# Second layer of six experts by Strassen's algorithm: seven block products in place of eight

## The chip, the cores and the metric

The kernel runs on one core of a Trainium2 chip. The metric is the device time of one execution in microseconds (us); smaller is better. In the profile's rows the engines are called PE (TensorE, matrix products) and PEld (its loading of stationary operands), DVE (VectorE), ACT (ScalarE), POOL (GpSimd) and SP (SyncE, which here only issues transfers).

## What is computed

Three stages follow each other. A gated linear attention over 4 batches of 8 heads, 768 steps and 48 channels gives x, 3072 rows of 384. The first mixture sends every row through all 8 experts. The second mixture sends each row through its top two of 8 experts. The change touches the first mixture:

```python
def _moe_ref(x, w_gate, w1, w2):          # x: 3072 x 384, w1: 8 x 384 x 1024, w2: 8 x 1024 x 384
    logits = x @ w_gate
    ...
    out = np.zeros((N, D), dtype=np.float32)
    for e in range(E):
        h = np.maximum(x @ w1[e], 0.0)
        ye = h @ w2[e]
        out += P[:, e:e + 1] * ye
    return out.astype(np.float32)
```

P is a table of 3072 x 8 weights, made from the logits by repeated normalising of rows and columns.

## The kernel before

Every fp32 operand of an expert is held as two fp16 parts, high and low, and a product a·b is summed from three matmuls in fp32: high·high, high·low and low·high. So each 128-deep step of a product is three matmuls, and every matmul loads a stationary operand of its own.

The first mixture runs expert by expert (e = 0 to 7), and in each expert over 6 blocks (nb) of 512 rows. A block has two parts. The first layer, `g1` (L130 to L133), makes the hidden values of 128 channels f for the 512 rows: 9 matmuls of 512 columns into one PSUM bank (L130), then ACT writes the high part of the rectified result (`hh`, L132) and DVE the low part (`hl`, L133). There are 8 such units to a block. The second layer, `g2` with `mm2` (L161), takes 128 rows at a time: 24 matmuls of 384 columns (8 channel groups by 3) into one bank, with hidden values as the stationary operand; then DVE multiplies by the row's weight in `Pm` and adds to `acc` in SBUF (L179). There are 4 such units to a block, and they are written between the `g1` units of the next block, so that PE has other work while ACT and DVE finish a block's hidden values. PSUM is one pool of 8 banks, which is used in turn.

Weights come in 7 pieces for each expert: SP issues a load of 512 KB or 384 KB into a staging tile `wst` (L86, L90), ACT makes the high part (L101) and DVE the low part (L102). `w_queue` lists these steps, and `w_pump` takes one of them whenever the planner's clock, which `pump(t)` moves by the time that the author set for each unit, is 2.2 past the last. `w_need` takes all that are left before an expert begins. POOL does nothing for experts 1 to 6.

Expert 0 of the first mixture is partly interleaved with the attention. During expert 7 the rows of x are written to DRAM for the second mixture, which gathers rows by expert; its first layer is L676, its second is `mm2` again, its transposes are L665, and its results are scattered to the output by POOL (L688). Each engine works through its own instructions strictly in the order in which they are written.

## Time and profile before

| | |
|---|---|
| median of 3 runs | 2121.61 us (2121.56 to 2124.22) |
| profiled execution | 2124.83 us, of which the span of instructions 2122.8 us |
| granted TensorE clock, mean | 0.994 |
| PE busy in the span | 2065.0 us (97%) |
| DVE, ACT, POOL busy | 898.8, 564.5, 248.0 us |

A busy time is the union of the times of an engine's instructions. Matmuls are pipelined, so the duration of one matmul is longer than its share of the engine; what one costs is read from the distance between starts.

### The profile page before, as it was taken

What the parts mean: (1) busy time and instruction counts of PE and PEld (TensorE: products, weight loads), DVE (VectorE), ACT (ScalarE), POOL (GpSimd) and SP (SyncE); (2) the same over time, 40 slices, a digit from 0 to 9 for tenths busy, and PEclk for the clock granted to TensorE, in tenths of its full rate; (3) what the DMA queues carried; (4) which work ended last, traced back from release to release, by engine and by line L of the source; (5) the groups of instructions that cost most, each with busy time, mean ns of one, the idle gap of its engine ahead of it and who ended that gap; (6) DMA issues with size and microseconds to landing.
All of it is one profiled execution on the core that took longest, in us unless ns stands there. A gap on an engine that the chain in (4) does not pass through costs nothing. (4 is left out here: it accounts for less than half of the span.)

```text
span 2122.8 us, 31270 instructions
## 1 busy us (share of the span) xinstructions
PE 2065.0 (97%) x13531; PEld 1196.5 (56%) x13531; DVE 898.8 (42%) x1697; ACT 564.5 (27%) x965; POOL 248.0 (12%) x236
## 2 busy tenths in 40 slices
PE   6999999999999999999999999999999999999996
PEld 5888655555555555555555555555555555555553
DVE  8889664232322322232232223223336655444431
ACT  5554412111211211121121112112333434332320
POOL 2434200000000000000000000000000232333332
PEclk9999999999999999999999999999999999999998
DMA  6332112100200100020010001001001435344431
GB/s 209 109 99 95 55 38 100 73 1 1 75 1 1 50 10 1 1 60 1 1 49 11 1 1 50 1 1 47 24 23 52 124 67 134 72 90 96 95 65 24
DMA packets 61820, 106.49 MB, mean 50 GB/s; under 512 B 10980, under 2 KB 44029, under 8 KB 61680
## 3 DMA queue, kind: packets, MB, share of 16 engines
q1 hardware_dynamic: 50256, 85.05, 12.6%
q0 software_dynamic: 11136, 18.89, 5.1%
q8 instruction: 107, 1.75, 0.3%
q10 hardware_dynamic: 288, 0.52, 0.1%
q14 instruction: 33, 0.27, 0.0%
HBM read 85.17 MB, written 21.63 MB: 50 GB/s over the span
## 5 line engine op out<-in xcount | busy, mean ns | idle before, releaser
L161 PE MATMUL bank<-wh,hh 128*128 128x384 f16 (+1 forms) x1984 | 647.6, 326 | 0.0
L161 PE MATMUL bank<-wl,hh 128*128 128x384 f16 (+1 forms) x1984 | 647.6, 326 | 0.0
L161 PE MATMUL bank<-wh,hl 128*128 128x384 f16 (+1 forms) x1984 | 647.5, 326 | 0.0
L161 PEld LDWEIGHTS <-hh 128*128 128x128 f16 (+1 forms) x3968 | 385.0, 98 | 264.7 <-issue 3.7
L132 ACT ACTIVATE hh<-bank 128x512 f16<-128x512 f32 x352 | 210.2, 597 | 1062.2 <-PE bank L130 1061.3
L133 DVE SCALAR_TENSOR_TENSOR hl<-bank,hh 128x512 f16<-128x512 f32 x352 | 243.2, 691 | 514.4 <-ACT hh L132 514.1
L130 PE MATMUL bank<-xl,wh 128*128 128x512 f16 x1056 | 400.2, 379 | 0.0
L130 PE MATMUL bank<-xh,wh 128*128 128x512 f16 x1056 | 400.2, 379 | 0.0
L130 PE MATMUL bank<-xh,wl 128*128 128x512 f16 x1056 | 400.2, 379 | 0.0
L130 PEld LDWEIGHTS <-wh 128*128 128x128 f16 x2112 | 206.3, 98 | 228.7
L161 PEld LDWEIGHTS <-hl 128*128 128x128 f16 (+1 forms) x1984 | 195.0, 98 | 128.0 <-issue 0.5
L179 DVE SCALAR_TENSOR_TENSOR acc<-bank,Pm,acc 128x384 f32<-128x384 f32 x168 | 103.7, 617 | 369.1 <-PE bank L161 369.0
L130 PEld LDWEIGHTS <-wl 128*128 128x128 f16 x1056 | 103.3, 98 | 124.6
L964 POOL MEMSET acc<- 128x768 f16 x8 | 5.9, 737 | 1276.7 <-DVE x L501 1276.7
L678 ACT ACTIVATE hh<-bank 128x384 f16<-128x384 f32 (+1 forms) x128 | 66.3, 518 | 238.1 <-PE bank L676 232.9
L688 POOL DMA_INDIRECT out_dram<-acc,ix x56 | 94.3, 1684 | 284.2 <-DVE acc L687 235.3
L102 DVE SCALAR_TENSOR_TENSOR wl<-wst,wh 128x768 f16<-128x768 f32 (+1 forms) x112 | 118.7, 1068 | 19.7 <-ACT wh L101 17.7
L679 DVE SCALAR_TENSOR_TENSOR hl<-bank,hh 128x384 f16<-128x384 f32 (+1 forms) x128 | 75.3, 589 | 118.6 <-ACT hh L678 108.9
L676 PEld LDWEIGHTS <-wh 128*128 128x128 f16 x768 | 72.6, 98 | 55.9 <-issue 3.7
L101 ACT ACTIVATE wh<-wst 128x768 f16<-128x768 f32 (+1 forms) x112 | 100.9, 927 | 3.5 <-DMA wst<-in_moe_w_dram 3.5
L676 PE MATMUL bank<-xh,wh 128*128 128x448 f16 (+1 forms) x384 | 98.8, 339 | 1.4 <-ACT xh L666 1.4
L676 PE MATMUL bank<-xl,wh 128*128 128x448 f16 (+1 forms) x384 | 98.9, 339 | 0.0
(178 smaller groups left out, 1516.1 us busy)
## 6 DMA issues: line engine op xcount, KB each, us to landing
wst<-in_moe_w_dram SPq DMA_DIRECT2D x48, 512.0 KB
wst<-in_moe_w_dram SPq DMA_DIRECT2D x64, 384.0 KB
la<-in_alpha_dram SPq DMA_DIRECT2D x24, 260.0 KB
lk<-in_k_dram SPq DMA_DIRECT2D x24, 256.0 KB
lq<-in_q_dram SPq DMA_DIRECT2D x22, 256.0 KB
lv<-in_v_dram SPq DMA_DIRECT2D x24, 192.0 KB
out_dram<-zero SPq DMA_DIRECT2D x6, 768.0 KB
xd<-x SPq DMA_DIRECT2D x24, 192.0 KB
```

The source lines that it names most:

```text
L101: nc.scalar.activation(t[0][:, s], st[:, :n], AF.Copy, scale=SW)
L102: nc.vector.scalar_tensor_tensor(t[1][:, s], st[:, :n], SW, t[0][:, s], op0=OP.mult, op1=OP.subtract)
L130: nc.tensor.matmul(p, w1s(e, a, kc, f), x[:, kc, s], start=(n == 0), stop=(n == 3 * KC - 1))
L132: nc.scalar.activation(hh[:, f, :], p, AF.Relu)
L133: nc.vector.scalar_tensor_tensor(hl[:, f, :], p, 0.0, hh[:, f, :], op0=OP.max, op1=OP.subtract)
L161: nc.tensor.matmul(p, a[:, f, s], w2s(x, b, f), start=(f + n == 0), stop=(f == FC - 1 and n == 2))
L179: nc.vector.scalar_tensor_tensor(acc[:, T, :], p, Pm[:, T, e:e + 1], acc[:, T, :], op0=OP.mult, op1=OP.add)
L676: nc.tensor.matmul(p, w1s(x, a, kc, f), xt[:, b * KC + kc, :], start=(i == 0), stop=(i == 3 * KC - 1))
L678: nc.scalar.activation(hh[:, f, :n], p, AF.Relu)
L679: nc.vector.scalar_tensor_tensor(hl[:, f, :n], p, 0.0, hh[:, f, :n], op0=OP.max, op1=OP.subtract)
L688: nc.gpsimd.indirect_dma_start(out=out, out_offset=bass.IndirectOffsetOnAxis(ap=ix, axis=0), in_=y, in_offset=None, bounds_check=N - 1, oo ...
L964: nc.gpsimd.memset(r, 0.0)
```

## The change

For experts 1 to 6 (`STR`) the second layer of a block of 512 rows is done as one product of 2 x 2 blocks. The hidden values A of the block are cut in halves of 256 rows and halves of 512 channels (A11, A12, A21, A22), the weights B in halves of 512 channels and of 192 columns. Seven products of sums of blocks (Winograd's form of Strassen's algorithm) give the same output as the eight products of blocks. The sums of A (S1 to S4) are made in the new first layer `s1`, those of B (T1, T3, T2N, N4) in `w_sums` once for each expert.

- `s1` does for a pair of channel groups (j and j + 4) what two `g1` units did, and then makes four sums: DVE forms them in fp32 straight from PSUM, ACT rounds all four to the high part in one instruction of 1024 elements, and POOL makes the low part with one subtraction of 1024 elements.
- `s2` does 7 products for each of 2 groups of rows, 12 matmuls of 192 columns each (4 channel groups by 3). The sums of products are formed by accumulating further products in the same bank and adding the bank to `acc` in between: 5 additions for each group. The banks are of a new pool of 4 (`long`); the other 4 stay for `s1`.
- `s2` of a block is written as one piece behind the first `s1` of the next block.
- The weight steps are three units deep in place of two (load, sums on POOL, split), spaced 6.0 on the planner's clock in the first mixture, with a staging tile twice as often reused (2 tiles in place of 3), and the low and high parts of a w2 piece are 1344 wide in place of 768.
- To make room, hidden values, staging of expert 0 and some tiles of the attention lie elsewhere in SBUF, the setup of the second mixture (`m2_setup`) stands in expert 7 in place of the end of the attention, and the zero writes (`zq`) stand in expert 7.

```diff
+    STR = range(1, E - 1)
+    ND = DM // 2
+    B11, B21, B22, T1, T3, T2N, N4 = range(7)
...
+    def w_sums(x, i, st):
+        if x not in STR or i < KC:
+            return
+        g = nc.gpsimd
+        b = st[:, :4 * ND].rearrange("p (a b d) -> p a b d", a=2, b=2)
+        c = [st[:, k * ND:(k + 1) * ND] for k in range(8)]
+        g.tensor_sub(st[:, 4 * ND:6 * ND].rearrange("p (a d) -> p a d", a=2), b[:, :, 1, :], b[:, 0, :, :])
+        g.tensor_sub(c[6], c[4], c[3])
+        g.tensor_add(c[7], c[2], c[6])
...
+    A11, A12, A22, S1, S2, S3, S4 = range(7)
+    def s1(e, nb, j, between):
...
+        for f in (j, j + FC // 2):
+            p = bank([128, 512])
+            n = 0
+            for kc in range(KC):
+                for a, x in ((0, xh), (0, xl), (1, xh)):
+                    nc.tensor.matmul(p, w1s(e, a, kc, f), x[:, kc, tok], start=(n == 0), stop=(n == 3 * KC - 1))
+                    n += 1
+            b.append(p)
+            if f == j:
+                t = SS["pool"].tile([128, 5, 256], F32, name="ss")
+                a11, a21 = p[:, :256], p[:, 256:]
+                nc.scalar.activation(left(e, nb, j, 0, A11), a11, AF.Relu)
+                nc.scalar.activation(t[:, 0], a21, AF.Relu)
+                stt(left(e, nb, j, 1, A11), a11, left(e, nb, j, 0, A11), OP.subtract)
+                stt(t[:, 3], a11, t[:, 0], OP.subtract)
+                between(1.97)
+        a12, a22 = p[:, :256], p[:, 256:]
+        nc.scalar.activation(lefts(e, nb, j, 0, A12, 2), p, AF.Relu)
+        stt(t[:, 1], a22, t[:, 0], OP.add)
+        stt(t[:, 2], a11, t[:, 1], OP.subtract)
+        stt(t[:, 4], a12, t[:, 2], OP.add)
+        stt(lefts(e, nb, j, 1, A12, 2), p, lefts(e, nb, j, 0, A12, 2), OP.subtract)
+        sums = t[:, 1:].rearrange("p a n -> p (a n)")
+        nc.scalar.activation(lefts(e, nb, j, 0, S1, 4), sums, AF.Copy)
+        nc.gpsimd.tensor_sub(lefts(e, nb, j, 1, S1, 4), sums, lefts(e, nb, j, 0, S1, 4))
+        between(1.97)
+    def s2(e, nb, Pm, between):
...
+        def prod(out, q, aop, wop, start=False, stop=False):
+            n = 0
+            for j in range(FC // 2):
+                for a, b in ((0, 0), (0, 1), (1, 0)):
+                    nc.tensor.matmul(out, left(e, nb, j, a, aop)[:, q * 128:(q + 1) * 128], w2t(e, b, wop, j),
...
+            a, c = long_bank([128, DM]), long_bank([128, DM])
+            BA[q], BC[q] = a, c
+            t, u = TT[q]
+            prod(a[:, Rt], q, A11, B11, start=True)
+            add(t, 0, ND, a[:, Rt])
+            prod(c[:, L], q, A22, N4, start=True)
+            prod(c[:, Rt], q, S1, T1)
+            add(u, 0, DM, c)
+        for q in range(2):
+            a, (t, u) = BA[q], TT[q]
+            prod(a[:, Rt], q, S2, T2N)
+            prod(a[:, L], q, A12, B21)
+            add(t, 0, DM, a)
+        for q in range(2):
+            a, c, (t, u) = BA[q], BC[q], TT[q]
+            prod(c[:, Rt], q, S4, B22, stop=True)
+            add(t, ND, ND, c[:, Rt])
+            prod(a[:, Rt], q, S3, T3, stop=True)
+            add(u, 0, DM, a[:, None, Rt].to_broadcast([128, 2, ND]))
...
-        for i in range(NW + 1):
+        for i in range(NW + 2):
             def f(i=i):
+                if i > 1:
+                    w_split(x, i - 2, st_.pop((x, i - 2)))
+                if 0 < i <= NW:
+                    w_sums(x, i - 1, st_[x, i - 1])
                 if i < NW:
                     st_[x, i] = w_load(x, i)
-                if i > 0:
-                    w_split(x, i - 1, st_.pop((x, i - 1)))
...
-            w_at[0] = clk[0] + 2.2
+            w_at[0] = clk[0] + (6.0 if len(W) < E else 2.2)
```

How the order on PE changes is seen where a first-layer unit of an expert of the first mixture meets the second layer of the block ahead. Before (`wh`, `wl` are the two parts of the weights, `hh`, `hl` those of the hidden values):

```order
L130 MATMUL bank<-xh,wl_7045 128x512
L161 LDWEIGHTS hh
L161 MATMUL bank<-wh_7044,hh 128x384
L161 LDWEIGHTS hh
L161 MATMUL bank<-wl_7045,hh 128x384
L161 LDWEIGHTS hl
L161 MATMUL bank<-wh_7044,hl 128x384
```

After (`wt` holds all parts and sums of the weights, `hid` all parts and sums of the hidden values):

```order
L272 MATMUL bank<-xh,wt_72 128x512
L306 LDWEIGHTS hid
L306 MATMUL long<-wt_72,hid 128x192
L306 LDWEIGHTS hid
L306 MATMUL long<-wt_72,hid 128x192
L306 LDWEIGHTS hid
L306 MATMUL long<-wt_72,hid 128x192
```

Each matmul still has a load of its own ahead of it. Before, 24 such pairs follow each other and then 18 of the first layer; now 168 pairs of half the width follow each other and then 72 of the first layer.

On DVE, one second layer of a block and the first layer of the next, before (two `g1` units, then one addition, four times over):

```order
L133 SCALAR_TENSOR_TENSOR hl<-bank,hh 128x512 x2
L179 SCALAR_TENSOR_TENSOR acc<-bank,Pm,acc 128x384
L133 SCALAR_TENSOR_TENSOR hl<-bank,hh 128x512 x2
L179 SCALAR_TENSOR_TENSOR acc<-bank,Pm,acc 128x384
L133 SCALAR_TENSOR_TENSOR hl<-bank,hh 128x512 x2
L179 SCALAR_TENSOR_TENSOR acc<-bank,Pm,acc 128x384
```

After: the last `s1` of a block (j = 3), the first of the next block (j = 0), and the ten additions of the `s2` between:

```order
L295 SCALAR_TENSOR_TENSOR hid<-bank,hid 128x256
L295 SCALAR_TENSOR_TENSOR ss<-bank,ss 128x256 x4
L295 SCALAR_TENSOR_TENSOR hid<-bank,hid 128x512
L295 SCALAR_TENSOR_TENSOR hid<-bank,hid 128x256
L295 SCALAR_TENSOR_TENSOR ss<-bank,ss 128x256 x4
L295 SCALAR_TENSOR_TENSOR hid<-bank,hid 128x512
L316 SCALAR_TENSOR_TENSOR acc<-long,Pm,acc 128x192
L316 SCALAR_TENSOR_TENSOR acc<-long,Pm,acc 128x384
L316 SCALAR_TENSOR_TENSOR acc<-long,Pm,acc 128x192
L316 SCALAR_TENSOR_TENSOR acc<-long,Pm,acc 128x384 x3
L316 SCALAR_TENSOR_TENSOR acc<-long,Pm,acc 128x192
L316 SCALAR_TENSOR_TENSOR acc<-long,Pm,acc 128x384
```

On POOL, which before has no row between the setup of the second mixture and its first gathers, the subtractions of `s1` (L291, four to a block) now stand with the sums of the weights (L127 to L129, four times for each expert) among them:

```order
L291 TENSOR_TENSOR hid<-ss,hid 128x1024 x9
L127 TENSOR_TENSOR wst<-wst 128x384
L128 TENSOR_TENSOR wst<-wst 128x192
L129 TENSOR_TENSOR wst<-wst 128x192
L127 TENSOR_TENSOR wst<-wst 128x384
L128 TENSOR_TENSOR wst<-wst 128x192
L129 TENSOR_TENSOR wst<-wst 128x192
L291 TENSOR_TENSOR hid<-ss,hid 128x1024
L127 TENSOR_TENSOR wst<-wst 128x384
L128 TENSOR_TENSOR wst<-wst 128x192
L129 TENSOR_TENSOR wst<-wst 128x192
L291 TENSOR_TENSOR hid<-ss,hid 128x1024 x2
```

The nine subtractions are the two blocks 0 and 1 and the first `s1` of block 2; the first two groups of weight sums so stand in the `s2` behind it, the third between j = 1 and j = 2 of block 2, the fourth behind its j = 3.

## Rows read from the trace of the kernel before

**Rows 1.** The profile's first part: busy us, share of the span, instructions.

```profile
PE 2065.0 (97%) x13531; PEld 1196.5 (56%) x13531; DVE 898.8 (42%) x1697; ACT 564.5 (27%) x965; POOL 248.0 (12%) x236
```

**Rows 2.** Busy time of the engines in an attention stretch, experts 1 to 6, second mixture.

```profile
core 0: us, PE busy (x) PEld busy (x) DVE busy (x) ACT busy (x) POOL busy (x), PEclk, DMA share, GB/s
50.00:100.00 50.00, 47.81 (x649) 40.66 (x646) 43.85 (x69) 25.22 (x52) 19.26 (x20) 1.00 0.32 101
300.00:1400.00 1100.00, 1100.00 (x5936) 580.84 (x5935) 335.66 (x500) 202.98 (x324) 0.00 (x0) 1.00 0.07 24
1600.00:2050.00 450.00, 441.55 (x3084) 265.39 (x3083) 228.85 (x619) 157.59 (x260) 138.00 (x103) 1.00 0.39 92
```

**Rows 3.** PE's timeline about one second-layer unit: start us, duration us; 24 L161 between.

```profile
1004.65 0.38 PE L130 MATMUL bank<-xh,wl 128*128 128x512 f16 x1
1004.87 0.33 PE L161 MATMUL bank<-wh,hh 128*128 128x384 f16 x1
...
1008.77 0.38 PE L130 MATMUL bank<-xh,wh 128*128 128x512 f16 x1
```

**Rows 4.** PE's timeline about one first-layer unit pair: 18 L130 up to 1004.87.

```profile
1000.99 0.38 PE L130 MATMUL bank<-xh,wh 128*128 128x512 f16 x1
```

**Rows 5.** PE's timeline in the attention: 18 L147 of 128 columns up to 31.19.

```profile
30.19 0.22 PE L147 MATMUL bank<-xh,wh 128*128 128x128 f16 x1
...
31.19 0.28 PE L271 MATMUL bank<-ident,ks 128*128 128x128 f32 x1
```

**Rows 6.** PEld groups: count, busy us, mean ns of one, idle before.

```profile
L161 PEld LDWEIGHTS <-hh 128*128 128x128 f16 x3840 | 371.6, 98 | 256.3 <-issue 1.2
L147 PEld LDWEIGHTS <-wl 128*128 128x128 f16 x240 | 24.0, 100 | 6.0 <-issue 3.8 <-DVE wl L102 0.5
```

**Rows 7.** DVE groups by shape, the same columns.

```profile
L133 DVE SCALAR_TENSOR_TENSOR hl<-bank,hh 128x512 f16<-128x512 f32 x352 | 243.2, 691 | 514.4 <-ACT hh L132 514.1
L179 DVE SCALAR_TENSOR_TENSOR acc<-bank,Pm,acc 128x384 f32<-128x384 f32 x168 | 103.7, 617 | 369.1 <-PE bank L161 369.0
L102 DVE SCALAR_TENSOR_TENSOR wl<-wst,wh 128x768 f16<-128x768 f32 x64 | 60.6, 954 | 5.6 <-ACT wh L101 4.0
L292 DVE TENSOR_TENSOR am<-acc,am 128x1024 f16<-128x1024 f32 x24 | 29.2, 1218 | 13.0 <-ACT am L291 12.9
L153 DVE SCALAR_TENSOR_TENSOR hl<-bank,hh 128x256 f16<-128x256 f32 x16 | 6.4, 410 | 0.0
L383 DVE TENSOR_TENSOR Pm<-Pm,rs 128x192 f32<-128x192 f32 x8 | 2.9, 358 | 0.3
```

**Rows 8.** ACT groups by shape.

```profile
L132 ACT ACTIVATE hh<-bank 128x512 f16<-128x512 f32 x352 | 210.2, 597 | 1062.2 <-PE bank L130 1061.3 <-PE bank L569 0.9
L101 ACT ACTIVATE wh<-wst 128x768 f16<-128x768 f32 x64 | 51.5, 835 | 1.5 <-DMA wst<-in_moe_w_dram 1.5
L291 ACT ACTIVATE am<-acc 128x1024 f16<-128x1024 f32 x24 | 25.4, 1056 | 19.7 <-POOL acc L284 19.7
L152 ACT ACTIVATE hh<-bank 128x256 f16<-128x256 f32 x16 | 6.2, 385 | 8.3 <-PE bank L147 8.2
```

**Rows 9.** POOL groups by shape.

```profile
L258 POOL TENSOR_TENSOR g<-acc,ce 64x192 f32<-64x192 f32 x40 | 45.7, 1143 | 99.1 <-DVE ce L247 68.4 <-PE bank L271 24.5 <-PE bank L305 4.7
L489 POOL IOTA vv<- 128x192 bf16 x1 | 0.7, 669 | 0.0
L467 POOL IOTA irow<- 128x128 bf16 x1 | 0.2, 238 | 0.0
```

**Rows 10.** POOL's one-input instruction of 512 elements, L284: ns least/median/most.

```profile
L284 POOL TENSOR_SCALAR_AFFINE_SELECT acc<-acc x48: 629/719/1643, 11.3 to 236.1; 128x512 f32<-128x512 f32 x48
```

**Rows 11.** What PE waited for from 1600 to 2050 us: total us, times, longest.

```profile
PE bank L665 <- DMA acc<-xd,ix: 5.5, 7, 1.6
PE bank L629 <- DVE rhs L622: 1.6, 1, 1.6
PE bank L676 <- ACT xh L666: 1.4, 1, 1.4
```

More of the change, by code (lines that the diff above doesn't have):

```diff
@@ L188 @@
     C2 = C + 2
-    LQ = [ap_.tile([128, NP, C], F32, name=f"lq{i}") for i in range(NL)]
+    spare = SPARE[0].bitcast(F32)
+    LQ = [spare[:, i * NP * C:(i + 1) * NP * C].rearrange("p (r c) -> p r c", r=NP) for i in range(NL)]
     LK = [ap_.tile([128, NP, C], F32, name=f"lk{i}") for i in range(NL)]
@@ L192 @@
     NV = 3
-    LV = [ap_.tile([128, H, D], F32, name=f"lv{i}") for i in range(NV)]
+    lv = [spare[:, NL * NP * C + i * H * D:NL * NP * C + (i + 1) * H * D] for i in range(2)]
+    lv.append(HID[:, 2 * FC * 512:2 * FC * 512 + 2 * H * D].bitcast(F32))
+    LV = [x.rearrange("p (h d) -> p h d", h=H) for x in lv]
     order = [(c, b) for c in range(NC) for b in range(B)]
@@ L748, in overflow @@
             for i in range(4):
-                st = sg.tile([128, 1024], F32, tag="wst", name="wst")
+                st = stage()
                 for a in range(2):
@@ L809 @@
                 gq += [("g2", e, nb, j) for j in range(4)]
+        elif e in STR:
+            stream.append(("s1", e, nb, 0))
+            stream += gq
+            gq = [("s2", e, nb)]
+            stream += [("s1", e, nb, j) for j in range(1, FC // 2)]
+        elif e and not nb:
+            stream += [("g1", e, nb, f) for f in range(3)] + gq + [("plain",)]
+            stream += [("g1", e, nb, f) for f in range(3, FC)]
+            gq = [("g2", e, nb, j) for j in range(4)]
         else:
@@ L850 @@
     actx.close()
-    wp2 = ctx.enter_context(tc.tile_pool(name="wts2", bufs=1))
-    m2_setup()
+    late = ctx.enter_context(tc.tile_pool(name="late", bufs=1))
+    WT.append(late.tile([128, 2 * W1N + 2 * W2N], F16, name="wt1"))
+    SPARE.append(WT[1][:, WPL:])
+    SG["pool"] = ctx.enter_context(tc.tile_pool(name="stage", bufs=2))
+    sctx = ExitStack()
+    SS["pool"] = sctx.enter_context(tc.tile_pool(name="sums", bufs=2))
     chains = []
@@ L975 @@
             pump(0.98 * g[2])
-        elif g[0] == "g1":
+        elif g[0] == "plain":
+            sctx.close()
+            banks(8, 0)
+            m2_setup()
+        elif g[0] == "s2":
+            need("sk%d" % (len(sks) - 1))
+            s2(*g[1:], Pm, pump)
+        elif g[0] in ("g1", "s1"):
             e, nb, f = g[1:]
```

195 lines of the change are left out of this document (144 added, 51 removed).

## The prediction

> **What bounds the kernel now.** I read the busy times first, then the windows by stage, then PE's timeline inside the stage, and last the groups of each engine by shape. PE is busy for 97% of the span [rows 1], and in the stretch of experts 1 to 6 for all of it, while DVE has 31%, ACT 18% and POOL nothing [rows 2]. A busy share does not say that PE works at its best pace, so the next thing to look at is the distance between starts. In the second layer 24 matmuls of 384 columns take from 1004.87 to 1008.77, 162.5 ns each [rows 3]; in the first, 18 of 512 columns take 3.88 us, 215.6 ns each [rows 4]. In the attention 18 matmuls of 128 columns, each with a weight load of its own, take 1.00 us, 55.6 ns each [rows 5]. These three lie on one line, 2.3 ns and 0.417 ns for each column. So PE is bound by columns, with hardly a cost for each matmul, and all that shortens the column count of this stage shortens the program, as long as the other engines keep up. The clock is 1.00 throughout that stage [rows 2].
>
> **The products.** For each block the change takes away 96 matmuls of 384 columns: 96 x 162.5 ns = 15.60 us. It adds 7 x 2 x 12 = 168 matmuls of 192 columns. No row has that width with fp16 operands; the line from 128 to 384 columns gives 55.6 + 64 x 0.417 = 82.3 ns. Its lower bound is half of the 384-column price, 81.3 ns; its upper bound is the mean weight load, 98 to 100 ns [rows 6], if loads did not overlap each other. I take 82.3, since the 128-column run stands well below 98 ns with the same kind of load. Then 168 x 82.3 = 13.83 us, and a block saves 1.77 us. There are 6 x 6 = 36 blocks: 63.8 us. The first layer's 72 matmuls of a block stay (15.52 us), so a block becomes 29.35 us long.
>
> A rule of the skill speaks against this step. The pace above comes from rows in which each matmul of 128 columns waits 55.6 ns for the next although the loads beside it last 100 ns each. The Trainium skill (TensorE: Matmul & The Clock Gate, section LDWEIGHTS) puts a load at its columns over 1.2 GHz, some 107 ns for 128. If that paced every pair, a block's second layer would take 168 x 107 ns = 17.9 us and the program would be about 84 us slower; by the rows it is 64 us faster. By that rule the 128-column run could not have happened, so this trace does not agree that a load paces its pair.
>
> **What the other engines get.** Durations are those of the same shapes. DVE has per `s1` five instructions of 256 (410 ns) and one of 512 (691 ns) [rows 7]: 11.0 us per block. The additions are six of 384 (617 ns) and four of 192, at most 410 ns: 5.3 us. The weights' low parts are 3 pieces of 1024 and 4 of 1344 an expert, at 1.2 ns an element 10 us, or 1.7 us per block. Together 18 of 29.35 us. ACT has 2 x 385 + 597 + 1056 ns per `s1` [rows 8], 9.7 us per block, and 1.5 us of weights: 11.2 us. Neither is a bound by throughput.
>
> By order they can still be late. The tightest addition is the one to `acc` after the product A12 B21, which must have read its bank before S3 T3 writes it: three products lie between, 3.0 us, against 0.6 us for the addition and at most 1.4 us for a weight piece ahead of it. The two banks of an `s1` are wanted again one `s1` later, 3.9 us, and are read out after 3 x 410 + 691 ns = 1.9 us. The waits are covered, and I put them at nothing.
>
> **The one price that the trace lacks** is POOL's subtraction of 1024 elements, x. It is the last link of a chain: after PE's last first-layer matmul of j = 3, which ends 0.16 us after its slot (0.38 less 0.216 us), DVE makes three sums (1.23 us), ACT rounds them (1.06 us), and POOL subtracts. PE reads the result in the last matmul of the third product. Until then it has 18 first-layer matmuls of the next block (3.88 us), two products (1.98 us) and 11 matmuls (0.91 us): 6.77 us. That leaves 6.77 - 0.16 - 2.29 = 4.3 us for one subtraction. But j = 1, 2 and 3 come 3.88 us apart, so above that POOL falls behind: 3x must fit in 4.3 + 2 x 3.88, so x may be 4.0 us. Beyond that PE waits 3(x - 4.0) in each block, and the gain of 1.77 us is gone at x = 4.6 us.
>
> The bounds for x are far apart. From below: the one-input instruction of 512 elements takes 629 ns at least [rows 10], so 1.3 us. From above: the only two-input one, 192 elements in 1143 ns [rows 9], so 6.1 us. The upper one works on runs of 48 elements with a broadcast operand; and short runs cost POOL much: 192 elements that lie apart, in groups of 24, take 669 ns, 128 in one run 238 [rows 9]. The new subtraction has one run of 1024 on all inputs, as the 512 row has runs of 128, so I count two input streams at that row's median, 4 x 719 ns = 2.9 us. At 2.9 us POOL has 11.6 us per block and no wait arises. The Trainium skill (GPSIMD Engine Reference, section 3.1) gives 4497 ns for a two-input add of 2048 fp32 elements; half of it is an estimate of 2.2 us, with which the sum would be the same.
>
> The weight sums (768 elements, by the same measure 2.2 us, four times an expert) stand between subtractions. One in each expert stands between j = 1 and j = 2 and pushes the two behind it by 2.9 + 2.2 - 3.88 = 1.2 us, so that the last is done about when PE wants it. I take 1 us for all experts.
>
> **What moves besides.** Before expert 1 the weight steps, 6.0 apart, are not through, and the rest is taken at once. ACT and DVE then hold the first `s1` up, but behind it stand four second-layer units of expert 0, 15.6 us of PE work: 0 to 10 us, I take 0, or 10 if that cover were gone. `m2_setup` makes ACT wait for a small transfer; 8 banks of 1.94 us hide that. The 16 zero writes now stand on SP's queue among x rows and weights in expert 7; the DMA share just before is 0.07 [rows 2], and the first gathers come long after: nothing. In the second mixture a staging tile is free for a load only when the split two pieces back is done (0.84 on ACT and 0.95 us on DVE [rows 7, 8]), so ACT may wait up to 1.8 us at each of 56 pieces. If all of it reached PE that were 100 us; but there PE waits for gathers and not for splits [rows 11], ACT is 35% busy, and 8 banks of 1.5 us lie between. I take 2 us.
>
> **Sum.** -63.8 + 1 + 2 = -60.8 us. The profiled execution took 2124.8 us, of which 2122.8 in the span, so its span becomes 2062; the median of the runs is 3.2 us under that execution, and 2121.6 - 60.8 = 2060.8 us.
>
> **Rivals.**
> - *POOL is late.* One mechanism, in the third product of each `s2`: from x = 4.6 us on the kernel is slower than before. At the upper bound of 6.1 us PE waits 6.3 us in each block, 36 x (6.3 - 1.8) = +162 us, 2284 us. For it speaks the only two-input row; against it its short runs. 0.11, of which 0.03 between 4.0 and 4.6, still faster.
> - *Weight loads pace PE.* At 98 ns each [rows 6] a block's second layer takes 16.5 us: 36 x 0.86 = +31 us, 2153 us. The 128-column run speaks against it, though it is only 18 long; over a longer stretch, 50 us of attention hold 649 matmuls, 77 ns each with many of them fp32 [rows 2]. 0.03.
> - *The change does not do what it says:* a 192-column matmul with its load costs about 92.9 ns (15.60 / 168), so that 168 of them take as long as the 96 before. Then 2122 us. No row speaks for it. 0.03.
> - *Losses at the seams* of 15 to 45 us, from weights that come late before expert 1 and in the second mixture, half of the bound above: 2075 to 2105 us. 0.06.
>
> **Chances and range.** My forecast, that the products are paid by column and nothing waits, has 0.77, and by itself lies between 2054 (81.3 ns a matmul and no losses: 36 x 1.95 = 70, less 2) and 2070 us. To leave out no more than 2 in 10 I take 2054 to 2090, which reaches into the seams' losses and the mild end of a late POOL. About 0.2% is what a measurement of this kernel can tell from no change. Faster by more than that: 0.77 + 0.06 + 0.03 = 0.86; within it 0.03; slower 0.08 + 0.03 = 0.11.
>
> **What would show it.** The products are right if 168 matmuls of L306 stand some 82 ns apart and PE still has no gaps in experts 1 to 6; weight loads as the bound would show as a distance near 98. A late POOL would show as PE idle before L306, released by POOL L291, inside the third product, and as a mean of L291 over 4 us. Seams would show as PE idle at the beginning of expert 1, or before the first-layer units of the second mixture with ACT or DVE as releaser. If x is near 4 us, or if the weight sums on POOL are far dearer than 2.2 us, the prediction is off by tens of us.

## The result: 19 us of the 61

The changed kernel takes 2102.43 us (median of four, 2100.86 to 2102.97), the kernel before 2121.59 (2121.15 to 2124.22) beside it: ratio 0.9906, 95% interval 0.9889 to 0.9923. It is faster by 19.2 us, not by the 60.8 of the forecast, and 12 us above the upper end of the range. The mechanism that was to bring the gain works; two thirds of what it brought is lost again in three places, by waits that the prediction put at 0 (1 with the sums of the weights), 0 and 2 us.

The profile's first part of the changed kernel, which answers [rows 1], and the three windows of [rows 2]:

```profile
PE 2016.1 (96%) x16123; PEld 1361.2 (65%) x16123; DVE 1229.3 (59%) x2513; ACT 725.8 (35%) x1277; POOL 625.4 (30%) x452
```

```profile
50.00:100.00 50.00, 47.43 (x642) 40.26 (x641) 43.84 (x69) 24.32 (x50) 19.28 (x20) 1.00 0.33 103
300.00:1400.00 1100.00, 1079.65 (x8640) 754.63 (x8639) 676.66 (x1334) 368.64 (x646) 373.28 (x209) 1.00 0.06 19
1600.00:2050.00 450.00, 435.11 (x2977) 260.87 (x2975) 215.71 (x565) 151.74 (x247) 137.29 (x102) 0.98 0.38 91
```

In experts 1 to 6 PE had no idle microsecond in 1100; now it has 20.4 there, and in the second mixture 14.9 of 450 instead of 8.5, at a lower clock. A window of 1100 us is too wide to show what happens in one block. PE's timeline about a block without a weight piece (the place of [rows 3, 4]; start, duration):

```profile
1013.93 0.38 PE L272 MATMUL bank<-xh,wt 128*128 128x512 f16 x1
1014.15 14.02 PE L306 MATMUL long<-wt,hid 128*128 128x192 f16 x168
1028.01 0.38 PE L272 MATMUL bank<-xh,wt 128*128 128x512 f16 x1
```

From 1014.15 to 1028.01 are 13.86 us, 82.5 ns a product; the forecast had 82.3. So the products are priced right, and weight loads (98 ns in the mean, as before [rows 6]) don't pace them. What took the gain away is in the list of PE's waits, which answers [rows 11] but for the whole span (total us, times, longest; the attention's waits and some short ones left out):

```profile
PE bank L851 <- DMA acc<-xd,ix: 10.1, 5, 2.8
PE long L306 <- DVE acc L316: 9.2, 8, 1.9
...
PE long L306 <- POOL hid L291: 4.8, 11, 1.6
...
PE bank L272 <- DVE ss L295: 3.8, 5, 0.8
...
PE bank L272 <- DVE acc L235: 2.5, 1, 2.5
```

Three of them lie inside experts 1 to 6 (L306 and L272), one at the opening of expert 1 (L235), one in the second mixture (L851). The 24 waits at L306 and L272 add up to 17.8 us. Each costs some 0.16 us more than is shown, because the last matmul ahead of it is shown to end that much behind its slot (0.246 less 0.0825 us at L306): 21.7 us, an estimate.

**Inside experts 1 to 6.** All waits stand in blocks in which a piece of the next expert's weights is prepared. One such stretch, first DVE, then POOL, then PE (start, duration, idle before and its releaser; where two shapes follow each other as "x2" the first is named, here 192 and then 1152 elements):

```profile
585.22 0.41 DVE L295 SCALAR_TENSOR_TENSOR ss<-bank,ss 128x256 f32<-128x256 f32 x1
585.55 3.24 DVE L146 SCALAR_TENSOR_TENSOR wt<-wst,wt 128x192 f16<-128x192 f32 x2
588.71 1.33 DVE L295 SCALAR_TENSOR_TENSOR ss<-bank,ss 128x256 f32<-128x256 f32 x3
...
596.06 3.24 DVE L146 SCALAR_TENSOR_TENSOR wt<-wst,wt 128x192 f16<-128x192 f32 x2
599.22 1.33 DVE L295 SCALAR_TENSOR_TENSOR ss<-bank,ss 128x256 f32<-128x256 f32 x3
600.46 0.68 DVE L295 SCALAR_TENSOR_TENSOR hid<-bank,hid 128x512 f16<-128x512 f32 x1
601.06 1.26 DVE L316 SCALAR_TENSOR_TENSOR acc<-long,Pm,acc 128x192 f32<-128x192 f32 x3
```

```profile
584.38 2.13 POOL L291 TENSOR_TENSOR hid<-ss,hid 128x1024 f16<-128x1024 f32 x1 [5.16 <-ACT hid L290]
586.46 1.12 POOL L127 TENSOR_TENSOR wst<-wst 128x384 f32<-128x384 f32 x1
587.65 1.58 POOL L128 TENSOR_TENSOR wst<-wst 128x192 f32<-128x192 f32 x1
589.32 0.59 POOL L129 TENSOR_TENSOR wst<-wst 128x192 f32<-128x192 f32 x1
...
594.88 2.13 POOL L291 TENSOR_TENSOR hid<-ss,hid 128x1024 f16<-128x1024 f32 x1 [1.54 <-ACT hid L290]
```

```profile
589.73 0.38 PE L272 MATMUL bank<-xh,wt 128*128 128x512 f16 x1 [0.76 <-DVE ss L295]
597.07 3.23 PE L306 MATMUL long<-wt,hid 128*128 128x192 f16 x37 [0.40 <-POOL hid L291]
601.52 2.72 PE L306 MATMUL long<-wt,hid 128*128 128x192 f16 x31 [1.23 <-DVE acc L316]
```

The reader is to see the low parts of a weight piece (L146) between the first and the second sum of an `s1`, and that they take 3.24 us. Behind them stand the other sums, so the banks are read out late (PE waits at 589.73), POOL's lower part starts late (it ends at 597.01, and PE waits for it until 597.07), and the additions, which come last in DVE's queue, are late too (601.52). In the block without a piece the first addition starts 2.7 us behind the first product, at 1016.84; here it starts 7.5 us behind, at 601.06:

```profile
1016.84 1.10 DVE L316 SCALAR_TENSOR_TENSOR acc<-long,Pm,acc 128x192 f32<-128x192 f32 x2
```

All the while POOL's instructions run beside the split, and those are longer as well: L128 takes 1.58 us, L129, of the same size and after the split has ended, 0.59.

**At expert 1.** PE stands still for 2.45 us before the first matmul of the first block, for the eviction L235 of the last tile of expert 0, which needs the last result of the normalisation. A stretch of lower clock follows: the mean granted clock is 0.89 from 310 to 325 us, 1.00 on either side. In the second line (columns as in [rows 2]) it is the third number from the end; the third line is the same stretch in e9 below, which has no such wait:

```profile
313.35 0.38 PE L272 MATMUL bank<-xh,wt 128*128 128x512 f16 x1 [2.45 <-DVE acc L235]
310.00:325.00 15.00, 12.55 (x62) 6.22 (x61) 9.95 (x19) 3.73 (x6) 4.91 (x4) 0.89 0.30 97
310.00:325.00 15.00, 15.00 (x91) 8.77 (x90) 8.43 (x14) 3.62 (x6) 4.84 (x4) 1.00 0.24 83
```

**In the second mixture**, the first matmul of the first layer and the last, in the kernel before and in the changed one (times of first and last start):

```profile
L676 PE MATMUL bank<-xh,wh x384: 322/344/363, 1645.0 to 2028.3; 128*128 128x384 f16 x96, 128*128 128x448 f16 x96
...
L676 PE MATMUL bank<-xl,wl x192: 325/340/353, 1671.1 to 2083.5; 128*128 128x384 f16 x96, 128*128 128x448 f16 x96
```

```profile
L862 PE MATMUL bank<-xh,wt x576: 322/352/528, 1613.3 to 2006.2; 128*128 128x384 f16 x96, 128*128 128x448 f16 x96
L862 PE MATMUL bank<-xl,wt x576: 323/338/363, 1639.0 to 2062.2; 128*128 128x384 f16 x96, 128*128 128x448 f16 x96
```

This took 438.5 us and now takes 448.9, 10.4 more for the same matmuls.

### The profile page after: what moved, and what is told of

Its sections match the earlier page's. It is cut to its first block, busy times and chain, and to the rows that moved or that the text cites. A ratio compares the mean times of both kernels' runs of the same rounds, so it can differ in the third digit from the quotient of the medians.

```text
span 2101.2 us, 38370 instructions
## 1 busy us (share of the span) xinstructions
PE 2016.1 (96%) x16123; PEld 1361.2 (65%) x16123; DVE 1229.3 (59%) x2513; ACT 725.8 (35%) x1277; POOL 625.4 (30%) x452
## 5 line engine op out<-in xcount | busy, mean ns | idle before, releaser
L272 PE MATMUL bank<-xh,wt 128*128 128x512 f16 x1728 | 521.9, 380 | 6.2 <-DVE ss L295 3.8
L306 PE MATMUL long<-wt,hid 128*128 128x192 f16 x6048 | 508.8, 246 | 14.1 <-DVE acc L316 9.2
L291 POOL TENSOR_TENSOR hid<-ss,hid 128x1024 f16<-128x1024 f32 x144 | 307.1, 2132 | 706.1 <-ACT hid L290 651.7
L306 PEld LDWEIGHTS <-hid 128*128 128x128 f16 x6048 | 499.6, 98 | 27.0 <-issue 11.1
L272 PEld LDWEIGHTS <-wt 128*128 128x128 f16 x2592 | 253.1, 98 | 306.2 <-PE bank L272 6.1
L225 PE MATMUL bank<-wt,hid 128*128 128x384 f16 (+1 forms) x2496 | 430.5, 328 | 1.8 <-DVE hid L866 1.8
L225 PEld LDWEIGHTS <-hid 128*128 128x128 f16 (+1 forms) x2496 | 242.2, 99 | 156.6 <-issue 5.2
L272 PE MATMUL bank<-xl,wt 128*128 128x512 f16 x864 | 328.2, 380 | 0.0
L316 DVE SCALAR_TENSOR_TENSOR acc<-long,Pm,acc 128x192 f32<-128x192 f32 (+1 forms) x360 | 187.3, 533 | 169.8 <-PE long L306 167.5
L295 DVE SCALAR_TENSOR_TENSOR ss<-bank,ss 128x256 f32<-128x256 f32 x576 | 241.5, 421 | 58.3 <-ACT hid L284 39.6
L146 DVE SCALAR_TENSOR_TENSOR wt<-wst,wt 128x1024 f16<-128x1024 f32 (+3 forms) x129 | 167.2, 1308 | 36.9 <-ACT wt L144 36.1
L862 PEld LDWEIGHTS <-wt 128*128 128x128 f16 x1152 | 110.9, 98 | 86.4 <-issue 4.7
L194 PE MATMUL bank<-xh,wt 128*128 128x512 f16 x384 | 120.0, 379 | 0.7 <-DVE acc L316 0.7
L862 PE MATMUL bank<-xh,wt 128*128 128x384 f16 (+1 forms) x576 | 109.1, 343 | 0.9 <-ACT xh L852 0.9
L284 ACT ACTIVATE hid<-bank 128x512 f16<-128x512 f32 x144 | 86.0, 597 | 66.4 <-PE bank L272 66.4
```

The source lines that it names most:

```text
L146: nc.vector.scalar_tensor_tensor(t[:, o + o1:o + o1 + n], src, SW, t[:, o:o + n], op0=OP.mult, op1=OP.subtract)
L194: nc.tensor.matmul(p, w1s(e, a, kc, f), x[:, kc, s], start=(n == 0), stop=(n == 3 * KC - 1))
L225: nc.tensor.matmul(p, h(a, f, s), w2s(x, b, f), start=(f + n == 0), stop=(f == FC - 1 and n == 2))
L272: nc.tensor.matmul(p, w1s(e, a, kc, f), x[:, kc, tok], start=(n == 0), stop=(n == 3 * KC - 1))
L291: nc.gpsimd.tensor_sub(lefts(e, nb, j, 1, S1, 4), sums, lefts(e, nb, j, 0, S1, 4))
L295: nc.vector.scalar_tensor_tensor(out, p, 0.0, x, op0=OP.max, op1=op)
```

## The experiments

My theory was that the weight pieces hold up `s1` and the additions, because the split stands ahead of them on DVE (order) and because DVE and POOL keep each other waiting (exclusion); that the reopened pools cost the seam; and that the two staging tiles cost the second mixture. The rivals were a chain inside the block that is too long by itself, a late POOL, and a loss in the second mixture that has nothing to do with staging. "Products" is the time from the first L306 to the last (36 blocks), "mixture 2" from the first L862 to the last, both in the profiled execution; a line number may stand a few higher in an experiment. Each code cut shows the lines that matter; "..." marks what is left out.

| kernel | us, median | ratio to before, 95% interval | products | mixture 2 |
|---|---|---|---|---|
| changed kernel | 2102.4 | 0.9906 (0.9889 to 0.9923) | 1067.3 | 448.9 |
| e1 no sums, no splits | 2077.2 | 0.9792 (0.9775 to 0.9808) | 1046.6 | 446.1 |
| e2 no low parts | 2077.7 | 0.9783 (0.9767 to 0.9799) | 1046.9 | 446.2 |
| e3 no sums | 2091.9 | 0.9851 (0.9834 to 0.9867) | 1059.7 | 449.3 |
| e4 three stages | 2088.8 | 0.9840 (0.9823 to 0.9856) | 1067.4 | 435.4 |
| e5 pools swapped | 2099.5 | 0.9896 (0.9880 to 0.9912) | 1067.4 | 446.0 |
| e6 pieces among products | 2089.2 | 0.9847 (0.9831 to 0.9862) | 1065.8 | 439.6 |
| e7 e4, e5, e6 together | 2084.6 | 0.9823 (0.9809 to 0.9837) | 1064.6 | 433.5 |
| e8 no sums, no L291 | 2080.0 | 0.9805 (0.9790 to 0.9821) | 1047.4 | 446.0 |
| e9 one ring of banks | 2094.3 | 0.9868 (0.9853 to 0.9883) | 1067.4 | 447.0 |
| e10 pieces kept apart | 2075.5 | 0.9781 (0.9766 to 0.9796) | 1044.7 | 446.7 |
| e11 e4, e9, e10 together | 2060.3 | 0.9710 (0.9696 to 0.9723) | 1044.7 | 435.3 |
| e12 one unit earlier | 2092.2 | 0.9859 (0.9844 to 0.9874) | 1067.5 | 441.9 |

Not all expectations were met: e1, e2, e4 and e10 came out 1 to 2.4 us below the range that I had taken to be theirs, and e6 lies between its two ranges.

**e1, no weight work for experts 2 to 6.** The sums and both parts of the split are left out.

```
 def w_sums(x, i, st):
-    if x not in STR or i < KC:
+    if x not in STR or i < KC or x > 1:
         return
...
 def w_split(x, i, st):
+    if 2 <= x < E - 1:
+        return
```

> Experts 2 to 6 get no sums, no high and no low parts (their loads stay, and their products run on the weights left in the buffer). Theory A, the weight pieces of the next expert cause the stalls inside experts 1 to 6 (some 21 of the 27 us that TensorE loses there against its slots; 4 belong to the first bank of expert 1, 2 to expert 7's pieces): 2079 to 2085 us, the TensorE waits on the adds, on POOL's lower parts and on the sums of s1 all but gone outside expert 1's first block and expert 6. Rival B, the chain inside a block (eviction, sums, lower part on POOL, product) is too long by itself: 2098 to 2103 us, and the waits stay where blocks have no weight piece either.

Measured 2077.2 us, and the products lose 20.7 us of their length. The weight pieces are the cause, and the chain inside a block is short enough without them (rival B falls): of PE's waits at L306 and L272 in experts 2 to 6 only one of 1.6 us is left, in expert 6, where expert 7's pieces were kept.

**e2, no low parts.** The loop of L145 to L147 over `todo` runs over nothing for experts 2 to 6.

> Only the DVE part of a weight piece (its low parts) is left out for experts 2 to 6; POOL's sums and ScalarE's high parts stay. Theory A1, DVE's split stands ahead of the sums of s1 and of the adds in DVE's order: 2080 to 2088 us, about as without any piece. Rival A2, POOL's sums of the weights push its lower parts of s1 back: 2093 to 2102 us, with TensorE's waits on POOL staying near 4.8 us.

Measured 2077.7 us, the same as e1. POOL's sums and ACT's high parts cost nothing while DVE doesn't split; rival A2 falls. It also gives the price of POOL's sums when nothing stands against them. POOL's groups in the changed kernel and in e2, from 350 to 1590 us (count; busy, mean ns of one; idle before):

```profile
L128 POOL TENSOR_TENSOR wst<-wst 128x192 f32<-128x192 f32 x20 | 25.8, 1289 | 1.6
L127 POOL TENSOR_TENSOR wst<-wst 128x384 f32<-128x384 f32 x20 | 25.6, 1279 | 6.7 <-DMA wst<-in_moe_w_dram 6.7
L129 POOL TENSOR_TENSOR wst<-wst 128x192 f32<-128x192 f32 x20 | 12.7, 633 | 1.6
```

```profile
L127 POOL TENSOR_TENSOR wst<-wst 128x384 f32<-128x384 f32 x20 | 20.1, 1003 | 0.0
L129 POOL TENSOR_TENSOR wst<-wst 128x192 f32<-128x192 f32 x20 | 11.8, 591 | 1.6
L128 POOL TENSOR_TENSOR wst<-wst 128x192 f32<-128x192 f32 x20 | 11.8, 591 | 1.6
```

**e3, no sums; e8, no POOL reads at all.** Here the splits stay at their places, and POOL's part is taken away: first the sums alone (the split reads loaded halves of the same size), then L291 too (the last line of the diff, in e8 only).

```
-    if x not in STR or i < KC:
+    if x not in STR or i < KC or x > 1:
         return
...
+    if x in STR and i >= KC and x > 1:
+        todo[1] = (st[:, None, :2 * ND].to_broadcast([128, 3, 2 * ND]),) + todo[1][1:]
...
-    nc.gpsimd.tensor_sub(lefts(e, nb, j, 1, S1, 4), sums, lefts(e, nb, j, 0, S1, 4))
```

> Only POOL's three sums of a weight piece are left out for experts 2 to 6 (the split reads loaded halves in their place, of the same size); ScalarE's and DVE's splits stay where they are. Theory A1 with exclusion (a split and a POOL operation with two SBUF inputs take turns, so that the sums nearly double the split): the 1152-element split falls from 2.1 to 1.4 us except where s1's lower part on POOL meets it, and 2086 to 2095 us. Order alone (the split's own 1.35 us is what is late): 2097 to 2101 us. Rival A2 (POOL's own queue): 2082 to 2088 us.

> As without the three sums, and POOL's lower parts of the four sums of s1 are left out too (the products read old ones): POOL then reads nothing of SBUF in experts 1 to 6 while DVE splits; the splits stay where they stand. Every split takes its time alone (1.22 us for 1024, 1.35 for 1152, 0.35 for 192). If exclusion makes the whole of the loss: 2077 to 2081 us, as without splits. If order alone keeps a part: 2084 to 2090 us, with waits on the adds left in the blocks that hold a piece.

e3 took 2091.9 us, e8 2080.0. DVE's split groups tell why, in the changed kernel, in e3 and in e8 (350 to 1590 us):

```profile
L146 DVE SCALAR_TENSOR_TENSOR wt<-wst,wt 128x1152 f16<-128x1152 f32 x20 | 37.3, 1863 | 4.1 <-ACT wt L144 4.1
L146 DVE SCALAR_TENSOR_TENSOR wt<-wst,wt 128x1024 f16<-128x1024 f32 x21 | 36.3, 1730 | 5.0 <-ACT wt L144 5.0
...
L146 DVE SCALAR_TENSOR_TENSOR wt<-wst,wt 128x192 f16<-128x192 f32 x20 | 21.3, 1065 | 0.0
```

```profile
L152 DVE SCALAR_TENSOR_TENSOR wt<-wst,wt 128x1024 f16<-128x1024 f32 x21 | 36.3, 1726 | 4.5 <-ACT wt L149 4.5
...
L152 DVE SCALAR_TENSOR_TENSOR wt<-wst,wt 128x1152 f16<-128x1152 f32 x20 | 26.9, 1347 | 0.0
L152 DVE SCALAR_TENSOR_TENSOR wt<-wst,wt 128x192 f16<-128x192 f32 x20 | 22.2, 1109 | 0.0
```

```profile
L152 DVE SCALAR_TENSOR_TENSOR wt<-wst,wt 128x1152 f16<-128x1152 f32 x20 | 27.1, 1356 | 4.4 <-ACT wt L149 4.4
L152 DVE SCALAR_TENSOR_TENSOR wt<-wst,wt 128x1024 f16<-128x1024 f32 x21 | 25.7, 1224 | 4.5 <-ACT wt L149 4.4
...
L152 DVE SCALAR_TENSOR_TENSOR wt<-wst,wt 128x192 f16<-128x192 f32 x20 | 7.0, 348 | 0.0
```

With the sums gone, the 1152 elements, which had met them, fall from 1863 to 1347 ns; the 1024 and the 192, which meet L291, stay long. With L291 gone as well every shape has one price. The products then need 1047.4 us, 19.9 less than in the changed kernel and 2.7 more than in e10, so exclusion makes most of the loss, and 2.7 us are left for order. It is not a clean division: without L291 PE has no lower part of POOL's to wait for either, and a split of the right length might still have made one late. e10 settles the practical side.

**e6, pieces among the products.** A unit of the weight work is issued after the second and the fifth product of a block and none in `s1`. (The cut leaves out the line that keeps `w_pump` from issuing there, and one that joins the naming of the weight buffer to the first load, as in e12.)

```
+            np_[0] += 1
+            if np_[0] in (2, 5) and wq:
+                wq.pop(0)()
             between(0.99)
...
```

> All work of the pieces stays; for experts 2 to 7 a unit is issued only after the second and the fifth of the fourteen products of a tile block, none among the first-layer blocks. Theory A1 (the order on DVE): the sums of s1 no longer stand behind a split, 2079 to 2086 us. Rival, the adds of the products take the delay instead, through banks that the later products write again: 2090 to 2103 us, TensorE's wait on the adds above 9 us.

Measured 2089.2 us, 1 us below the range of the rival and 3 above that of the theory. The rival's mechanism is what the trace shows: the waits for `s1` are gone, but those of L306 for an addition rise from 9.2 to 16.5 us, and the products gain only 1.5 us. The splits were now beside the last L291 of the block and the sums of the next piece, and up to 2.37 us long. The rest of its gain lies elsewhere: 9.3 us in the second mixture, a side effect (e12), 2.8 ahead of expert 1 (see e11), and 1.7 because the lower clock behind expert 1's start did not show in its execution.

**e10, pieces kept apart.** The same place, but by POOL's times: ACT's high parts after product 4, one low part after product 7 and one after 9, each followed by the next load, and POOL's sums after 11.

```
...
+    def w_apart(n):
...
+        if n == 4:
+            AP["todo"] = sorted(i for y, i in st_ if y == x)
+            for i in AP["todo"]:
+                w_split(x, i, st_[x, i], low=False)
+        elif n in (7, 9):
+            if AP["todo"]:
+                i = AP["todo"].pop(0)
+                w_split(x, i, st_.pop((x, i)), high=False)
+            if AP["i"] < NW:
+                st_[x, AP["i"]] = w_load(x, AP["i"])
+                AP["i"] += 1
+        elif n == 11:
+            for y, i in sorted(st_):
+                w_sums(x, i, st_[x, i])
...
```

> All work of the pieces stays, for experts 2 to 7 among the products, and so that POOL and DVE don't meet: ScalarE's high parts after the fourth product, one low part after the seventh and one after the ninth (POOL's last lower part of s1 ended two products before), each followed by the next load, and POOL's sums after the eleventh, when the splits are done. If exclusion is the cause, the splits take their time alone (1.22 and 1.35 us), the adds have 3 products of slack, and it gives what leaving the pieces out gave, less nothing: 2077 to 2083 us. If any order of these pieces costs the adds or the sums their place, 2086 to 2092 us, as when they were moved among the products without this care.

Measured 2075.5 us, with nothing left out, and PE has no wait at L306 in experts 1 to 6. A stretch of its DVE and POOL shows the splits (x2: 192 and 1152) at 1.62 us instead of 3.24, between L291 and the sums:

```profile
616.93 1.62 DVE L146 SCALAR_TENSOR_TENSOR wt<-wst,wt 128x192 f16<-128x192 f32 x2
```

```profile
613.59 2.14 POOL L291 TENSOR_TENSOR hid<-ss,hid 128x1024 f16<-128x1024 f32 x1 [1.75 <-ACT hid L290]
622.22 1.00 POOL L127 TENSOR_TENSOR wst<-wst 128x384 f32<-128x384 f32 x1 [6.49 <-DMA wst<-in_moe_w_dram]
```

**e5, pools swapped; e9, one ring.** e5 opens the accumulating pool of expert 1 ahead of the other, so that the first block's banks are others (first diff); e9 (second diff) never reopens, and all banks come from one ring of eight.

```
+        if long:
+            PS["long"] = pst.enter_context(tc.tile_pool(name="psl", bufs=long, space=PSUM))
         PS["bank"] = pst.enter_context(tc.tile_pool(name="ps", bufs=main, space=PSUM))
-        if long:
-            PS["long"] = pst.enter_context(tc.tile_pool(name="psl", bufs=long, space=PSUM))
```

```
     def long_bank(shape, dt=F32):
-        return PS["long"].tile(shape, dt, tag="long", name="long")
+        return bank(shape, dt)
...
-                if e == 1:
-                    banks(4, 4)
...
-            banks(8, 0)
```

> Only the two bank pools of experts 1 to 6 trade places, so that the first block of expert 1 starts in a bank that an older eviction of expert 0 read, and not in the one that waits for the last scaled tile. Theory: the 2.45 us wait there and the half-clock window behind it go: 2097 to 2100 us. Rival, the sums of that first block queue behind the same work on DVE and the wait moves to the third and fourth bank: 2101 to 2104 us.

> One ring of eight banks all through: no pool is closed and opened again at expert 1 and at the second mixture, and the sums' banks and the accumulating ones take turns in it. Theory: the 2.4 us wait before expert 1's first block comes from the opening of new pools, which waits for the last eviction of the old one wherever its bank lies, and goes with it, and the half-clock window behind it too; the short waits of s1 for a bank (3.8 us) go as well: 2094 to 2099 us. Rival, DVE is itself late there (Sinkhorn, weight pieces) and the first block's sums wait as long: 2100 to 2103 us.

e5's time, 2099.5 us, was in the range I gave, but not for my reason: the wait stays, 2.39 us for the same L235 at 312.33, and the products and the stretch before them are no shorter. What it gains lies in the second mixture (446.0 against 448.9 us) and ahead of expert 1 (1.0 us). My reading, that one bank was an unlucky one, was wrong. In e9 the wait is gone, and the first product starts at 342.8 us, against 347.0 in e12, whose attention took as long and whose start of expert 1 is the changed kernel's: 4.2 us. The time is 2094.3; the rest of what it gains lies, in its profiled execution, ahead of expert 1 (2.9 us, see e11) and in the second mixture (1.9). So the reopening itself makes the first block wait for the last eviction, wherever its bank lies. The waits of L272 for a bank (3.8 us) went as well, but came back as waits of L306 for POOL (from 4.8 to 9.4 us): the products are as long as before.

**e4, three stages; e12, one unit earlier.** e4 gives the second mixture its old staging: three tiles of 1024 and the split one unit behind the load. e12 keeps the two tiles, and joins the naming of the weight buffer to the first load, so that all units of the second mixture stand one earlier.

```
         elif g[0] == "plain":
...
+            SG["pool"] = gctx.enter_context(tc.tile_pool(name="stage3", bufs=3))
+            SG["n"] = 1024
...
+        d = 2 if x < E else 1
-        for i in range(NW + 2):
+        for i in range(NW + d):
             def f(i=i):
-                if i > 1:
-                    w_split(x, i - 2, st_.pop((x, i - 2)))
+                if i >= d:
+                    w_split(x, i - d, st_.pop((x, i - d)))
...
```

```
-        wq.append(lambda: w_alloc(x))
+        if x < E:
+            wq.append(lambda: w_alloc(x))
...
             def f(i=i):
+                if i == 0 and x >= E:
+                    w_alloc(x)
```

> From the start of the second mixture's weights on, staging as in the kernel before: three tiles of 1024 and the split one unit behind its load; the first mixture as in the changed kernel. Theory C, the two tiles with the split two units behind cost the second mixture its 10.4 us: 2090 to 2094 us, TensorE's waits on the gathered rows back from 10.1 to about 5.5 us. Rival D, the second mixture's loss comes from its start (where the throttle and the expert's loads stand against the gathers) and not from the staging: 2099 to 2103 us.

> Only the naming of the next weight buffer, which took a unit of its own, is joined to the first load for the experts of the second mixture, so that every load and split there stands one unit (2.2 us of the kernel's own count) earlier. When the pieces were moved among the products this edit came with it and the second mixture lost 9 us less. If that was the cause: 2091 to 2096 us. If it was the first mixture's change: 2101 to 2103 us.

Measured 2088.8 and 2092.2 us; the second mixture takes 435.4 and 441.9 us, less than before the change in e4. PE's waits for gathered rows after 1580 or 1600 us fall from 10.1 to 4.7 and to 7.1 us. What moves is when a weight load meets the gathers. SP, POOL and PE in the changed kernel, then SP and POOL in e4, at the same expert:

```profile
1831.97 3.30 SPq L111 DMA_DIRECT2D wst<-in_moe_w_dram  x2
```

```profile
1834.62 1.24 POOL L842 DMA_INDIRECT acc<-xd,ix  x1 [0.30 <-PE bank L862]
```

```profile
1840.08 0.58 PE L851 MATMUL bank<-i,acc 128*128 128x128 f16 x6 [2.83 <-DMA acc<-xd,ix]
```

```profile
1821.48 5.38 SPq L111 DMA_DIRECT2D wst<-in_moe_w_dram  x3
...
1830.04 1.08 POOL L842 DMA_INDIRECT acc<-xd,ix  x1 [0.30 <-issue]
```

In e4 the loads are issued by 1826.9 and the gathers start at 1830; in the changed kernel loads go out at 1832 to 1835 and the gathers at 1834.6. Four gathers in 1826 to 1842 us land after a median of 4.1 us in the changed kernel and 3.1 us in e4. That the loads take the gathers' share of the DMA engines is argued from this; no run delays the loads alone.

The waits are only half of it. From 1580 us on all of PE's waits together are 14.8 us in the changed kernel, 11.0 in e12 and 7.1 in e4. The rest is the clock. In windows of 10 us from 1600 to 2060 the granted clock is below 1.00 in three stretches of the changed kernel (0.80 and 0.86 from 1650 to 1670, 0.83 from 1840 to 1850, 0.99 and 0.84 from 1950 to 1970), each with a wait of 2 to 2.9 us in it or just ahead of it, in one of e12 (0.66 from 1650 to 1660), and in none of e4. What is missing to 1.00, added up over the windows, is an estimate of 6.8 us for the changed kernel and 3.4 for e12. So waits and clock make 14.5 us between the changed kernel and e4, of which 13.5 were measured, and 7.3 between e12 and e4, of which 6.5 were. That two tiles are too few is not needed to explain the loss, since e12, which has two, is slower than e4 by no more than its waits and its one stretch of lower clock; a run that separates the number of tiles from the times of the loads was not made.

**e7 and e11, the sums.**

> Three stages in the second mixture, banks swapped, pieces among the products. If the three losses are separate they add: 2102.4 less 13.6 for the stages (measured), some 19 for the pieces and 4 for the banks, 2064 to 2069 us. If expert 1's first block only passes its wait on, 2068 to 2073. If time freed earlier is given back where the second mixture waits for its rows, 2075 or more.

> Pieces kept apart, one ring of banks, three stages in the second mixture: 2102.4 less 22 less 4 less 13.6 us if the three losses are separate, 2060 to 2067 us, near what the prediction had for the change. If time won before the second mixture is given back there, 2070 to 2078 us.

e7 took 2084.6 us. It was built on e5 and e6, of which neither did what I thought. The number is that of the third case, the reason is not: nothing is given back in the second mixture, which takes 433.5 us. e11, of the three parts that did, took 2060.3 us (2058.78 to 2062.39), 42.1 less than the changed kernel. Alone the three had given 13.6, 8.1 and 26.9 us, 48.6 together. Where the 6.5 us between are counted twice is seen in the profiled executions: the spans are shorter by 14.5 (e4), 10.0 (e9) and 29.3 us (e10), that of e11 by 44.2, which is 9.6 less than the sum. 3.6 of these lie ahead of expert 1, where the last matmul of the normalisation (L560) starts at 309.6 us in the changed kernel, 308.9 in e4, 306.7 in e9 and 306.9 in e10 and e11; most of it is there by the first L225 of expert 0, at 46.0 and 45.4, and at 43.1 to 43.4 in the other three. None of the edits touches that part of the program. The granted clock over the first 50 us is 0.90 in the changed kernel, 0.93 in e10 and 1.00 in e9, but 0.97 in e7, where the last L560 is as late as in the changed kernel (309.4); the cause is open. 1.6 of the 9.6 us are the lower clock at expert 1, which did not show in e10 either. Another 4.0 are the second mixture, which took 1.9 and 2.2 us less in e9 and e10 (two stretches of lower clock in place of three) before it was mended itself. In experts 1 to 6 of e11 PE waits for nothing; its windows of 1240 us in the changed kernel and in e11:

```profile
320.00:1560.00 1240.00, 1220.26 (x9619) 837.25 (x9617) 720.51 (x1405) 414.49 (x729) 379.54 (x227) 1.00 0.08 26
```

```profile
320.00:1560.00 1240.00, 1238.94 (x9787) 850.93 (x9786) 707.61 (x1483) 425.47 (x747) 359.40 (x227) 1.00 0.08 26
```

## Why the prediction was wrong

**Right.** 168 products take 13.86 us (13.83 forecast), and a block 29.40 us (29.35). POOL's subtraction, for which I took 2.9 us between 1.3 and 6.1, takes 2.132 us, and is not late by itself: e1 and e10 show no wait for it in blocks without a piece beside it, or with one kept apart. (Its slack was smaller than the 4.3 us that I had worked out: in the block at 1014.15 the last one starts at 1013.65, and the 36th product matmul, which reads its result, comes at 1017.0, 3.4 us later.) Loads don't pace PE. With the three losses removed (e11) the change is worth 62 us, and the time is the forecast's within 0.5 us. That it comes so close is luck in part: e11's second mixture takes 3.2 us less than that of the kernel before (435.3 against 438.5), where the forecast had 2 more, and its profiled span, 2057.0, is 5 us below the forecast of it.

**The step that failed** is the sentence on order, "The waits are covered, and I put them at nothing". It was wrong by 22.6 us (1067.3 less 1044.7 us of the products). I had worked out two covers: three products of slack for an addition behind at most 1.4 us of weight work, and 3.9 us for an `s1` whose banks are read out in 1.9 us. In the second I had put no weight piece ahead. The first was for the wrong addition. PE stands at 601.52 before the 73rd matmul of the `s2` (35 and 37 lie ahead), the seventh product, for the addition of the first product, A11 B11. That has five products of slack and not three, but it stands on DVE behind all sums of the `s1` ahead: it starts at 1016.84 in the block without a piece, where PE wants it done by 1020.1 (72 matmuls of 82.5 ns behind 1014.15), so that 2.8 us were left for a piece. In both covers I took the price of a split from a kernel where POOL did nothing beside it [rows 2, 7]. A piece of 192 and 1152 took 3.24 us, not 1.6; 1.9 and 3.24 us are more than 3.9, and so the banks, POOL and the additions were late one after the other. In e8, where the split has its own price and stands at the same place, 2.7 us are left for the order alone, with the caveat given there.

The sums of the weights, put at 1 us because they delay POOL, cost nothing by delaying POOL (e2) and 7.6 us by lengthening the split (e3). The row that bounded POOL's price from above [rows 9] was too high for these shapes: 192 elements with two inputs cost 591 ns here when DVE leaves POOL alone, not 1143 (those of [rows 9] are of another shape, and whether DVE has a part in their price was not tried).

**The seams.** "0 to 10 us, I take 0" for expert 1 was 2.45 us of waiting and about 1.7 us for the lower clock behind it (from the first L272 to the first L306 36.7 us, in e9 and e10 35.0 and 35.1). The reason was another than the one I weighed: not late weights, but the reopened pools (e9). For the second mixture I took 2 us, looked at ACT and the banks, and found that PE waits for gathers and not for splits. That was the right row [rows 11] with the wrong conclusion: it said where a change of the loads' times would be paid. It was 10.4 us, about half of them waits and half the lower clock behind them, which I had not counted at all.

**Together:** 22.6 less 1 for the pieces, 4.1 at expert 1, 10.4 less 2 in the second mixture, 1.8 for 36 blocks of 29.40 and 2.6 ahead of expert 1 (the last matmul of the normalisation, L387 before and L560 now, starts at 307.0 and 309.6), are 38.5 of the 39.2 us between the profiled span (2101.2) and the forecast of it (2062).

**The rivals.** "Losses at the seams of 15 to 45 us" held the time (2075 to 2105) with a chance of 0.06; the range stopped at 2090. (Its lower end, 2054, is called one without losses but counts 2 us of them.) Its seams were 12.5 us of the loss beyond the forecast; the greater part, inside the blocks, was in no rival, and a "late POOL" was foreseen only for a price above 4.0 us.

## What to carry to other kernels

When work moves to POOL, price DVE's and POOL's instructions that read two SBUF operands as one queue, and look for them side by side in the trace: a duration taken from a kernel with an idle POOL is a lower bound. When a stage becomes shorter, go through every instruction that stands in the same queue ahead of the new deadlines, and put background work where neither partner is at work (e10), not merely elsewhere (e6). A place where PE already waits for a transfer [rows 11] is where a shift of other loads by one unit of the weight work was paid here (e12).

## What was not expected of the hardware

**DVE and POOL take turns.** A DVE instruction with two SBUF inputs and a POOL instruction that reads two wait for each other, for a whole instruction: 1024 elements on DVE take 1.22 us alone (e8, e10) and 1.73 in the mean in the changed kernel; 192 take 0.35 and 1.07; 192 on POOL 0.59 and 1.29 in the mean (L128). L291 takes 2.12 to 2.14 us in all of its 144, so where a split met it, it was DVE that waited. The sums and additions on DVE, which read one operand from PSUM, keep their price beside POOL (421 and 614 ns in the changed kernel, 421 and 616 in e8, which has no L291).

The Trainium skill (SBUF — State Buffer, section SBUF: two separate sides) says so: the port pair that GpSimd and VectorE share is an exclusive lock, which a VectorE operation with two SBUF inputs needs against a GpSimd operation that reads SBUF, and whoever comes first holds it for the whole instruction. These runs agree.

**The clock can fall after a short wait.** The wait of 2.45 us at expert 1 was followed by a granted clock of 0.89 in the mean from 310 to 325 us, a stretch at 1.2 GHz in part (matmuls of L272 0.43 us apart there in place of 0.22); that of 2.83 us at 1840.08 by 0.83 from 1840 to 1850. It is not certain. Eleven of the profiled executions have the wait at expert 1 (2.3 to 2.5 us): in eight of them, the changed kernel, e1 to e5, e8 and e12, the clock was 0.89 from 310 to 325 us, in e6, e7 and e10 it was 1.00, and the wait of 2.57 us at 1900.29 in the changed kernel was followed by 1.00 too. In e9 and e11, which have no wait there, it was 1.00. What decides between them is open.
